# The first feed-forward layer of the last block as a 2x2 block product of seven multiplications, in the fused sliding-window attention and squared-ReLU kernel

## The chip, the cores and the metric

The kernel runs on one core of one Trainium2 chip. The metric is device time in microseconds (us) of one execution. The time before is 298.63 us, the median of 3 runs (298.5 to 298.88). The profile is of one more execution, which took 298.21 us; its span on the core's engines is 296.2 us, and the 2.0 us around the span are start and end of the program.

## The reference

`reference()` computes causal attention in a window of 64 positions, per head, then a feed-forward layer with a squared ReLU:

```python
scores = scale * np.matmul(q, k.transpose(0, 1, 3, 2))       # q, k, v: 8 batches, 8 heads, 576 positions, 64
scores = np.where((rel >= 0) & (rel < 64), scores, -1e9)     # rel = query position - key position
attn = softmax(scores); x = (attn @ v)                       # to 4608 tokens x 512
h = np.maximum(x @ w_in, 0.0)                                # w_in: 512 x 2048
out = (h * h) @ w_out                                        # w_out: 2048 x 512
```

Inputs and output are fp32; the kernel computes in fp16 with fp32 sums.

## The kernel before

The 4608 tokens are nine blocks of 512: block g takes positions 0 to 511 of batch g, and block 8 takes the last 64 positions of all eight batches. A block goes through three stages: attention in four units of two heads, which leaves its 512x512 input transposed in `xT[g]`; layer 1 (`F1`), which leaves the squared ReLU, features by tokens, in `h2[g]` (16 slices of 128 features); and layer 2, which writes the output. The stages of three blocks run beside each other: step n of the loop at L709 does layer 2 of block n, layer 1 of block n+1 and attention of block n+2. The order of every engine's queue is written out by hand: the body runs under `tc.manual_schedule()`, so each engine gets its instructions in program order, and it takes them one after the other.

**Layer 1** of a block is 16 calls of `F1` (L351). Each has four matmuls of 128x512 into one bank (L358, depth 512 in four chunks of 128), a maximum with zero on VectorE from the bank to an fp32 tile `hr` (L361), and a square on ScalarE into `h2` (L362). The banks are the two of the pool `ps_f1`, in turn.

**Layer 2** of blocks 2 to 8 is a 2x2 block product by seven multiplications already (`L2S`, L453), once for each half s of the tokens. A product p of 1 to 7 is eight matmuls of 128x256 (`product`, L446). Four sums of blocks of `h2` are formed for it by `S_sum` (L434, on VectorE at L422, 128x1024 fp16 each). Products add up in two banks: `chain` takes 1, 6, 7 and 4, one after the other, and `side` holds 2 in its left and 5 and 3 in its right half. After 1, 6, 5 and 4 ScalarE copies a result to the output tile (`scaled`, L460); after 2, 7 and 3 VectorE adds one to it (`plus`, L463). A product that goes on in `chain`, or starts anew in it, so waits until the copy or the addition before it has read the bank. In the last step (block 8) s=0 has the two `ps_f1` banks (`more`), and s=1 has `chain` and `side`.

**The order around the change.** For steps 1 to 8 a string (`order`, L726 to L728) says how calls of layer 1 ("1") and layer 2 ("2") follow each other; the resulting list is `fill`, and a place in it is called a position below. `put(i, work)` sets other work ahead of position i: sums, attention units, and so on (L733 to L761). Step 6 (layer 2 of block 6, layer 1 of block 7, attention of block 8) and step 7 (layer 2 of block 7, layer 1 of block 8, no attention) have 30 positions each, mostly "1" and "2" in turn. Step 8, the last, has only the 14 products of layer 2 of block 8. Sums that a step's first products need are formed at the end of the step before: `S_sum` 3 (position 20), 1 and 2 (positions 28 and 29) for s=0.

[...]

Of the kernel before, what the change touches and what calls it, by code (L numbers as in the profile page):

```python
# [8 lines left out]
FP32 = mybir.dt.float32  # L9
FP16 = mybir.dt.float16  # L10
# [5 lines left out]
def kernel(  # L16
# [314 lines left out]
    def X(g, hp, engine=nc.scalar, pool=ps_tr, tag="tr", own=None):  # L331

        if g not in xT:
            xT[g] = xtpool.tile([P, DMC, 512], FP16, name="xT", tag="xT")
        if g == B:
            nc.sync.dma_start_transpose(out=xT[g][:, hp, :].rearrange("p (j t) -> p j t", j=4),
                                        in_=xs[g, hp][:].rearrange("p j h d -> p (j h d)"))
            return
        if own is not None:
            tr = at_ps[own][:, 0, :].bitcast(FP16).rearrange("p (a b) -> p a b", a=2)  # L340
        else:
            tr = pool.tile([P, 2, 512], FP16, name="xtr", tag=tag)
        for jp in range(4):
            nc.tensor.transpose(out=tr[:, 0, jp * P:(jp + 1) * P], in_=xs[g, hp][:, jp, :, :],  # L344
                                identity=ident[:])
        copy(engine, xT[g][:, hp, :], tr[:, 0, :])
# [4 lines left out]
    def F1(g, f, pool=ps_f1, tag="f1", into=None):  # L351
        if g not in h2:
            h2[g] = h2pool.tile([P, FFC, 512], FP16, name="h2", tag="h2")
        hps, done = open_f1.pop((g, f), (None, 0))
        if hps is None:
            hps = into if into is not None else pool.tile([P, 512], FP32, name="hps", tag=tag)
        for c in range(done, DMC):
            nc.tensor.matmul(hps[:], w_in_sb[:, c, f * P:(f + 1) * P], xT[g][:, c, :],  # L358
                             start=(c == 0), stop=(c == DMC - 1))
        hr = opool.tile([P, 512], FP32, name="hr", tag="hr")  # L360
        nc.vector.tensor_scalar(out=hr[:], in0=hps[:], scalar1=0.0, scalar2=None, op0=ALU.max)  # L361
        nc.scalar.activation(out=h2[g][:, f, :], in_=hr[:], func=AF.Square)  # L362
# [58 lines left out]
    def minus(out, a, b, op=ALU.subtract, engine=None):  # L421
        (engine or nc.vector).tensor_tensor(out=out, in0=a, in1=b, op=op)  # L422
# [11 lines left out]
    def S_sum(g, k, s):  # L434
        if k == 1:
            minus(s_of(1, s), a_of(g, 1, 0, s), a_of(g, 1, 1, s), ALU.add)
        elif k == 2:
            minus(s_of(2, s), s_of(1, s), a_of(g, 0, 0, s))
        elif k == 3:
            minus(s_of(3, s), a_of(g, 0, 0, s), a_of(g, 1, 0, s))  # L440
        else:
            minus(s_of(4, s), a_of(g, 0, 1, s), s_of(2, s))

    def product(to, a, b, start):
        for f in range(HF):
            nc.tensor.matmul(to, a[:, f, :], b[:, f, :], start=start and f == 0, stop=f == HF - 1,  # L446
                             skip_group_check=True)

    def flush():
        while to_store:  # L450
            to_store.pop(0)()
# [65 lines left out]
    with tc.manual_schedule():  # L517
# [191 lines left out]
        for n in range(1, NBLK):  # L709
            g = seq[n]  # L710
            last = n == NBLK - 1
            one = None if last else seq[n + 1]
            if n == 1:
                second = [lambda ts=ts, i=i: F2(g, ts, i, None, None, into=(chain, side)[ts % 2])
                          for ts in range(4) for i in range(4)]
            elif last:
                more = [ps_f1.tile([P, 512], FP32, name="more", tag="f1") for _ in range(2)]
                banks = [(more[0][:, 0:HC], more[1]), (chain[:, 0:HC], side)]
                second = [lambda p=p, s=s: L2S(g, p, s, banks[s])
                          for p, s in ((1, 0), (2, 0), (1, 1), (6, 0), (2, 1), (5, 0), (7, 0),  # L720
                                       (6, 1), (3, 0), (4, 0), (5, 1), (7, 1), (3, 1), (4, 1))]
            else:
                second = [lambda p=p, s=s: L2S(g, p, s, (chain[:, 0:HC], side))
                          for s in range(2) for p in ORDER]
            first = [] if last else [lambda f=f: F1(one, f) for f in range(FFC)]
            order = ("22222222" + 8 * "112" if n == 1 else  # L726
                     "2" * 14 if last else
                     ("2112121212121211" if n == 2 else "1212121212121211") + "21212121121122")  # L728
            a, b = iter(first), iter(second)
            fill = [next(a if c == "1" else b) for c in order]  # L730
            at = {}

            def put(i, *work):  # L733
                at.setdefault(i, []).extend(work)

            if n == 1:
                put(0, lambda: Sc(g2, 3), lambda: A(g2, 2))
                put(2, lambda: M(g2, 3))
                put(3, lambda: X(g2, 2, own=1))
                put(5, lambda: A(g2, 3))  # L740
                put(7, lambda: X(g2, 3, own=1))
                for i, k in ((1, 1), (3, 2), (6, 3), (8, 4)):
                    put(i, lambda k=k: T_sum(k))
            else:
                for i, k, s in (((0, 1, 1), (0, 2, 1), (2, 4, 0), (3, 3, 1), (4, 4, 1)) if last else
                                ((2, 4, 0), (4, 1, 1), (6, 2, 1), (9, 3, 1), (18, 4, 1))):
                    put(i, lambda k=k, s=s: S_sum(g, k, s))
            if not last:
                end = len(fill) - 1
                put(24 if n == 1 else 20, lambda: S_sum(one, 3, 0))  # L750
                put(end if n == 1 else end - 1, lambda: S_sum(one, 1, 0))
                put(end, lambda: S_sum(one, 2, 0))
            base = 4 * (n + 2)
            for i, two in zip((11, 22) if n == 1 else (9, 20) if n == 2 else (9, 17) if n == 6 else (8, 19),
                              (units[base:base + 2], units[base + 2:base + 4])):
                for t, u in enumerate(two):
                    if u is not None:
                        put(i, lambda u=u, t=t: Sc(*u, i=t))
                        put(i + 3 + t, lambda u=u: M(*u))
                        put(i + 6, lambda u=u, t=t: A(*u, i=t))  # L760
                        put(i + (7 if u[0] == B else 8 + t), lambda u=u, t=t: X(*u, own=t))  # L761
            for i, group in enumerate(fill):
                for work in at.pop(i, []):
                    work()
                total = 12 + (30 * (n - 1) + i + 1) * (len(load_list) - 12) // 140
                while done < total and (parts_left or pending):
                    next_part()
                    done += 1
                group()
            assert not at, at.keys()  # L770
# [30 lines left out]
```

## Time and profile before

| what | value |
|---|---|
| profiled execution | 298.21 us, span 296.2 us |
| median of 3 runs | 298.63 us (298.5 to 298.88) |
| granted TensorE clock | 1.00 in every stage |
| step 7, 253.63 to 279.67 us | 26.04 us: TensorE busy 26.04, VectorE 18.05, ScalarE 12.37, GpSimd 0.00 |
| step 8, 279.67 to 292.06 us | 12.39 us: TensorE busy 12.39, VectorE 7.00, ScalarE 3.08, GpSimd 1.38 |
| tail, 292.06 to 296.2 us | 4.14 us: ScalarE 0.39, GpSimd 0.40, DMA |

The times of day in the text ("at 253.63") count from the start of the span. Steps are found in the trace by the matmuls: step 7 begins with the four matmuls into `hps` that follow product 4 of block 6, and step 8 with the first product into `more`. The profile's engines are PE (matmuls), PEld (loading of weights, beside PE), DVE (VectorE), ACT (ScalarE), POOL (GpSimd) and SP (the DMA queue). A line of a list of groups gives the line of the code, engine, operation, output and inputs with shapes and count, then total busy time and mean nanoseconds of one, then the idle time of the engine before them and who ended it. A line of a timeline gives start, length, engine, line and operation.

### The profile page before, as it was taken

To read this page: it belongs to the slowest core of one execution; us is meant where nothing else is said; L and a number is where in the kernel's file an instruction comes from. 1 tells how busy PE (TensorE), PEld (TensorE's weight loads), DVE (VectorE), ACT (ScalarE), POOL (GpSimd) and SP (SyncE) were. 2 spreads that over 40 slices of the span, in tenths; PEclk is the share of its full clock that TensorE was granted. 3 is DMA by queue.
4 is the path that set the end of the run, shared out by engine and by line. 5 is a ranking of instruction groups with operands and counts; after the bars stand their busy time and mean duration, and the time that the engine had idled before them with its cause. 6 is when DMAs were issued, how large, how long until landed. Compare 5 with 4: busy or idle time off the path is not lost.

```text
span 296.2 us, 7372 instructions
## 1 busy us (share of the span) xinstructions
PE 287.7 (97%) x2905; PEld 180.3 (61%) x2905; DVE 216.3 (73%) x379; ACT 170.3 (57%) x292; POOL 125.8 (42%) x215
## 2 busy tenths in 40 slices
PE   7899999999999999999999999999999999999994
PEld 5543545555445466667666766676667666766783
DVE  4677539588867787878778877987788679866651
ACT  3666757688366656565665566556655654444521
POOL 4668848984383267229425633913232000000002
PEclk9999999999999999999999999999999999999999
DMA  6999999999999995999999999799997023100015
GB/s 209 259 323 392 407 326 237 321 247 196 177 254 185 190 216 106 209 181 234 181 207 226 200 180 226 157 198 200 196 221 202 2 38 107 73 37 35 2 71 142
DMA packets 143650, 56.05 MB, mean 189 GB/s; under 512 B 127712, under 2 KB 136160, under 8 KB 143616
## 3 DMA queue, kind: packets, MB, share of 16 engines
q1 hardware_dynamic: 143232, 55.00, 85.2%
q0 software_dynamic: 144, 0.39, 0.6%
q8 instruction: 22, 0.36, 0.5%
q10 hardware_dynamic: 240, 0.20, 0.3%
q14 instruction: 12, 0.10, 0.1%
HBM read 38.80 MB, written 9.44 MB: 163 GB/s over the span
## 4 chain that ended last, share of the span: by engine, by line
PE 88%; SPq 5%; DMA 4%; POOL 1%; ACT 0%; issue 0%; DVE 0%
PE hps L358 39%; PE chain L446 16%; PE side L446 12%; PE ops L394 5%; DMA wsum<-in_moe_w_in_dram 4%; PE at L318 4%; PE at L288 3%; PE side L394 2%; PE chain L394 2%; SPq L180 2%; PE more L446 2%; PE at L344 2%; SPq L173 2%; PE tr L257 1%; SPq L132 1%; SPq L139 1%
## 5 line engine op out<-in xcount | busy, mean ns | idle before, releaser
L362 ACT ACTIVATE h<-hr 128x512 f16<-128x512 f32 x144 | 90.2, 630 | 92.5 <-DVE hr L361 92.1
L358 PE MATMUL hps<-xT,w_in_sb 128*128 128x512 f16 x560 | 138.6, 379 | 0.5 <-POOL w_in_sb L120 0.4
L361 DVE TENSOR_SCALAR hr<-hps 128x512 f32<-128x512 f32 x143 | 97.2, 687 | 42.6 <-PE hps L358 39.4
L358 PEld LDWEIGHTS <-w_in_sb 128*128 128x128 f16 x564 | 52.8, 98 | 48.1 <-POOL w_in_sb L120 1.9
L446 PEld LDWEIGHTS <-hsum 128*128 128x128 f16 x448 | 43.2, 98 | 13.2
L120 POOL CAST v_ev<-st_v 128x512 f16<-128x512 f32 x31 | 21.6, 696 | 45.3 <-DMA st_v<-in_v_dram 45.3
L446 PEld LDWEIGHTS <-h 128*128 128x128 f16 x336 | 32.7, 98 | 9.3
L120 POOL CAST k<-st_k 128x512 f16<-128x512 f32 x33 | 21.4, 651 | 38.2 <-DMA st_k<-in_k_dram 30.4
L295 ACT ACTIVATE pm<-at 128x1024 f16<-128x1024 f32 x35 | 34.1, 1014 | 2.1 <-PE at L288 2.1
L387 POOL DMA_DIRECT2D out_dram<-osb x3 | 1.8, 595 | 63.6 <-ACT osb L460 62.2
L446 PE MATMUL chain<-wsum,hsum 128*128 128x256 f16 x208 | 27.0, 273 | 0.0
L328 DVE TENSOR_TENSOR xs<-at,rden 128x512 f16<-128x512 f32 x36 | 24.9, 692 | 1.2
L302 DVE TENSOR_TENSOR pm<-pm,mask 128x1024 f16<-128x1024 f16 x32 | 23.7, 754 | 1.9 <-ACT pm L295 1.9
L422 DVE TENSOR_TENSOR hsum<-h 128x1024 f16<-128x1024 f16 x28 | 20.4, 728 | 5.4 <-ACT h L362 5.4
L233 POOL CAST v_od<-st_v 64x512 f16<-64x512 f32 x30 | 22.4, 748 | 1.6
L120 POOL CAST q<-st_q 128x512 f16<-128x512 f32 x28 | 19.2, 711 | 4.7 <-DMA qT<-q 2.1
L394 PEld LDWEIGHTS <-h 128*128 128x128 f16 x128 | 11.6, 98 | 12.2
L460 ACT ACTIVATE osb<-chain 128x256 f32<-128x256 f32 x39 | 14.5, 373 | 5.6 <-PE chain L446 5.6
L318 PEld LDWEIGHTS <-pm 128*64 128x64 f16 x576 | 11.2, 110 | 6.9 <-DVE pm L302 3.2
L118 ACT ACTIVATE xT<-at 128x512 f16<-128x512 f16 x22 | 12.8, 587 | 4.0 <-PE at L344 4.0
L394 PE MATMUL ops<-w_out_sb,h 128*128 128x512 f16 x64 | 14.8, 380 | 0.0
L318 PE MATMUL at<-v_ev,pm 128*64 128x65 f16 x384 | 13.8, 197 | 0.2 <-ACT v_ev L118 0.2
(91 smaller groups left out, 317.2 us busy)
## 6 DMA issues: line engine op xcount, KB each, us to landing
st_k<-in_k_dram SPq DMA_DIRECT2D x37, 256.0 KB, 3.7
out_dram<-osb SPq DMA_DIRECT2D x32, 256.0 KB, 2.8
st_q<-in_q_dram SPq DMA_DIRECT2D x29, 256.0 KB, 4.9
st_v<-in_v_dram SPq DMA_DIRECT2D x28, 256.0 KB, 4.1
w_st<-in_moe_w_in_dram SPq DMA_DIRECT2D x4, 512.0 KB, 5.9
wsum<-in_moe_w_in_dram SPq DMA_DIRECT2D x4, 512.0 KB, 9.8
hsum<-in_moe_w_out_dram SPq DMA_DIRECT2D x4, 512.0 KB, 7.9
wsum<-in_moe_w_out_dram SPq DMA_DIRECT2D x4, 512.0 KB, 9.2
```

Of the source, the lines that this page charges most:

```text
L120: engine.tensor_copy(out=out, in_=in_)
L233: nc.gpsimd.tensor_copy(out=od[g][to:to + 64, m, :, 0:D], in_=st["v", g, c][of:of + 64, :].rearrange("p (h d) -> p h d", h=H))
L295: nc.scalar.activation(out=p[:, hh, :] if apart else p[:], in_=sc[hh] if apart else both[:], func=AF.Exp, scale=1.0 / float(D) ** 0.5)
L302: nc.vector.tensor_tensor(out=p[:], in0=p[:], in1=m.unsqueeze(1).broadcast_to([P, 2, 512]), op=ALU.min)
L318: nc.tensor.matmul(a[jj * 64:(jj + 1) * 64, hh, jp * VW:jp * VW + D + 1], pm[g, hp][:, hh, j * 64:(j + 1) * 64], vsel, start=True, stop=True)
L328: nc.vector.tensor_tensor(out=x[:].rearrange("p j h d -> p h j d"), in0=a[:, :, :, 0:D], in1=rden[:].unsqueeze(3).broadcast_to([P, 2, 4, D ...
L358: nc.tensor.matmul(hps[:], w_in_sb[:, c, f * P:(f + 1) * P], xT[g][:, c, :], start=(c == 0), stop=(c == DMC - 1))
L361: nc.vector.tensor_scalar(out=hr[:], in0=hps[:], scalar1=0.0, scalar2=None, op0=ALU.max)
L362: nc.scalar.activation(out=h2[g][:, f, :], in_=hr[:], func=AF.Square)
L394: nc.tensor.matmul(f2[g, ts][:], h2[g][:, f, ts * P:(ts + 1) * P], w_out_sb[:, f, :], start=(f == 0), stop=(f == FFC - 1))
L422: (engine or nc.vector).tensor_tensor(out=out, in0=a, in1=b, op=op)
L446: nc.tensor.matmul(to, a[:, f, :], b[:, f, :], start=start and f == 0, stop=f == HF - 1, skip_group_check=True)
```

## The change

Layer 1 of block 8, in step 7, becomes a 2x2 block product: features in two halves i, depth (the 512 inputs) in two halves k, tokens in two halves j of 256. It needs four sums of blocks of `w_in` (`W_sum`, each two operations of 128x1024 fp16) and four of blocks of `xT` (`X_sum`, 128x512 fp16). W sums 1 and 2 are formed on GpSimd and sum 3 on VectorE, in step 6; X sum 1 in step 6, the others and W sum 4 in step 7, on VectorE.

A product p is made for one m of 0 to 3 at a time, which stands for two of the eight slices of 128 features of each half: four matmuls of 128x256 into one bank (`product1`). So there are 28 calls of `L1S`, in step 7's string "112" fourteen times, 42 positions: position 3k and 3k+1 hold product number k for two m side by side, and position 3k+2 a product of layer 2. Positions 0 to 20 are m of 0 and 1, positions 21 to 41 are m of 2 and 3, with products in the order 5, 1, 2, 6, 7, 3, 4.

Each m has three banks, a and b in its `at_ps` tile and c from `ps_f1`; even and odd m have different ones. Partial sums go from bank to bank by copies on ScalarE: product 5 in b is copied to SBUF (`kept5`), product 1 in a is copied to b, a takes product 2 on top and is finished (VectorE maximum, ScalarE square, `done`), b takes 6 and is copied to c, c takes 7, is copied to a, and is finished with `kept5` added; b takes 3 and is finished with `kept5` added; a takes 4 and is finished. To finish with `kept5` (`done5`) is an addition on VectorE, a maximum on GpSimd, and a square on GpSimd, or on ScalarE for the block (0, 1) of m 2 and 3.

In step 8 the second and third products change places ((1, 1) stands ahead of (2, 0), as p and s), and the sums of `h2` are formed in another order; sum 3 for s=0 of block 8 is formed in step 8, no more in step 7.

```diff
@@ -445,6 +445,93 @@
         for f in range(HF):
             nc.tensor.matmul(to, a[:, f, :], b[:, f, :], start=start and f == 0, stop=f == HF - 1,
                              skip_group_check=True)
+
+    wsums, xsums = {}, {}
+    HX = 256
+
+    def w_of(i, k):
+        return w_in_sb[:, 2 * k:2 * k + 2, i * HF * P:(i + 1) * HF * P]
+
+    def x_of(g, k, j):
+        return xT[g][:, 2 * k:2 * k + 2, j * HX:(j + 1) * HX]
+
+    def W_sum(k, engine, cc):
+        if k not in wsums:
+            t = tpool.tile([P, HP, 512], FP16, name="wS", tag="T")
+            wsums[k] = t[:].rearrange("p a b -> p (a b)").rearrange("p (c f) -> p c f", c=2)
+        a, b, op = {1: (w_of(1, 0), w_of(1, 1), ALU.add), 2: (wsums.get(1), w_of(0, 0), ALU.subtract),
+                    3: (w_of(0, 0), w_of(1, 0), ALU.subtract), 4: (w_of(0, 1), wsums.get(2), ALU.subtract)}[k]
+        minus(wsums[k][:, cc, :], a[:, cc, :], b[:, cc, :], op, engine)
+
+    def X_sum(g, k):
+        if k not in xsums:
+            t = apool.tile([P, 2, 512], FP16, name="xS", tag="pm", bufs=4)
+            xsums[k] = t[:, 0, :].rearrange("p (c t) -> p c t", c=2)
+        a, b = {1: (x_of(g, 0, 1), x_of(g, 0, 0)), 2: (x_of(g, 1, 1), xsums.get(1)),
+                3: (x_of(g, 1, 1), x_of(g, 0, 1)), 4: (x_of(g, 1, 0), xsums.get(2))}[k]
+        minus(xsums[k], a, b)
+
+    def product1(to, m, a, b, start):
+
+        for u in range(2):
+            f = (2 * m + u) * P
+            for cc in range(2):
+                nc.tensor.matmul(to[:, u * HX:(u + 1) * HX], a[:, cc, f:f + P], b[:, cc, :],
+                                 start=start and u == 0 and cc == 0, stop=cc == 1, skip_group_check=True)
+
+    kept5 = {}
+
+    def L1S(g, p, m, banks):
+
+        if g not in h2:
+            h2[g] = h2pool.tile([P, FFC, 512], FP16, name="h2", tag="h2")
+        a, b, c = banks
+
+        def h_of(i, j):
+            return h2[g][:, i * HF + 2 * m:i * HF + 2 * m + 2, j * HX:(j + 1) * HX]
+
+        def piece32(name):
+            return stp.tile([P, 512], FP32, name=name, tag="st")
+
+        def done(i, j, bank):
+            hr = piece32("ls")
+            nc.vector.tensor_scalar(out=hr[:], in0=bank, scalar1=0.0, scalar2=None, op0=ALU.max)
+            nc.scalar.activation(out=h_of(i, j), in_=hr[:].rearrange("p (u t) -> p u t", u=2), func=AF.Square)
+
+        def done5(i, j, bank):
+            y = piece32("ls")
+            nc.vector.scalar_tensor_tensor(out=y[:], in0=bank, scalar=1.0, in1=kept5[m][:],
+                                           op0=ALU.mult, op1=ALU.add)
+            nc.gpsimd.tensor_scalar(out=y[:], in0=y[:], scalar1=0.0, scalar2=None, op0=ALU.max)
+            y = y[:].rearrange("p (u t) -> p u t", u=2)
+            if m < 2 or j == i:
+                nc.gpsimd.tensor_tensor(out=h_of(i, j), in0=y, in1=y, op=ALU.mult)
+            else:
+                nc.scalar.activation(out=h_of(i, j), in_=y, func=AF.Square)
+
+        if p == 5:
+            product1(b, m, wsums[1], xsums[1], True)
+            kept5[m] = piece32("p5")
+            copy(nc.scalar, kept5[m][:], b)
+        elif p == 1:
+            product1(a, m, w_of(0, 0), x_of(g, 0, 0), True)
+            copy(nc.scalar, b, a)
+        elif p == 2:
+            product1(a, m, w_of(0, 1), x_of(g, 1, 0), False)
+            done(0, 0, a)
+        elif p == 6:
+            product1(b, m, wsums[2], xsums[2], False)
+            copy(nc.scalar, c, b)
+        elif p == 7:
+            product1(c, m, wsums[3], xsums[3], False)
+            copy(nc.scalar, a, c)
+            done5(1, 1, c)
+        elif p == 3:
+            product1(b, m, wsums[4], x_of(g, 1, 1), False)
+            done5(0, 1, b)
+        else:
+            product1(a, m, w_of(1, 1), xsums[4], False)
+            done(1, 0, a)
 
     def flush():
         while to_store:
@@ -717,14 +804,22 @@
                 more = [ps_f1.tile([P, 512], FP32, name="more", tag="f1") for _ in range(2)]
                 banks = [(more[0][:, 0:HC], more[1]), (chain[:, 0:HC], side)]
                 second = [lambda p=p, s=s: L2S(g, p, s, banks[s])
-                          for p, s in ((1, 0), (2, 0), (1, 1), (6, 0), (2, 1), (5, 0), (7, 0),
+                          for p, s in ((1, 0), (1, 1), (2, 0), (6, 0), (2, 1), (5, 0), (7, 0),
                                        (6, 1), (3, 0), (4, 0), (5, 1), (7, 1), (3, 1), (4, 1))]
             else:
                 second = [lambda p=p, s=s: L2S(g, p, s, (chain[:, 0:HC], side))
                           for s in range(2) for p in ORDER]
-            first = [] if last else [lambda f=f: F1(one, f) for f in range(FFC)]
+            apart = n == NBLK - 2
+            if apart:
+                cs = [ps_f1.tile([P, 512], FP32, name="c", tag="f1") for _ in range(2)]
+                three = [(at_ps[i][:, 0, :], at_ps[i][:, 1, :], cs[i][:]) for i in range(2)]
+                first = [lambda p=p, m=m: L1S(one, p, m, three[m % 2])
+                         for two in ((0, 1), (2, 3)) for p in (5, 1, 2, 6, 7, 3, 4) for m in two]
+            else:
+                first = [] if last else [lambda f=f: F1(one, f) for f in range(FFC)]
             order = ("22222222" + 8 * "112" if n == 1 else
                      "2" * 14 if last else
+                     "112" * 14 if apart else
                      ("2112121212121211" if n == 2 else "1212121212121211") + "21212121121122")
             a, b = iter(first), iter(second)
             fill = [next(a if c == "1" else b) for c in order]
@@ -742,13 +837,15 @@
                 for i, k in ((1, 1), (3, 2), (6, 3), (8, 4)):
                     put(i, lambda k=k: T_sum(k))
             else:
-                for i, k, s in (((0, 1, 1), (0, 2, 1), (2, 4, 0), (3, 3, 1), (4, 4, 1)) if last else
+                for i, k, s in (((1, 3, 0), (2, 1, 1), (3, 2, 1), (4, 4, 0), (6, 3, 1), (8, 4, 1)) if last else
+                                ((4, 4, 0), (8, 1, 1), (12, 2, 1), (17, 3, 1), (30, 4, 1)) if apart else
                                 ((2, 4, 0), (4, 1, 1), (6, 2, 1), (9, 3, 1), (18, 4, 1))):
                     put(i, lambda k=k, s=s: S_sum(g, k, s))
             if not last:
                 end = len(fill) - 1
-                put(24 if n == 1 else 20, lambda: S_sum(one, 3, 0))
-                put(end if n == 1 else end - 1, lambda: S_sum(one, 1, 0))
+                if not apart:
+                    put(24 if n == 1 else 20, lambda: S_sum(one, 3, 0))
+                put(end if n == 1 or apart else end - 1, lambda: S_sum(one, 1, 0))
                 put(end, lambda: S_sum(one, 2, 0))
             base = 4 * (n + 2)
             for i, two in zip((11, 22) if n == 1 else (9, 20) if n == 2 else (9, 17) if n == 6 else (8, 19),
@@ -759,6 +856,16 @@
                         put(i + 3 + t, lambda u=u: M(*u))
                         put(i + 6, lambda u=u, t=t: A(*u, i=t))
                         put(i + (7 if u[0] == B else 8 + t), lambda u=u, t=t: X(*u, own=t))
+            if n == NBLK - 3:
+                for i, k, engine in ((18, 1, pool), (18, 2, pool), (27, 3, dve)):
+                    for cc in range(2):
+                        put(i + (cc if engine is dve else 0), lambda k=k, e=engine, cc=cc: W_sum(k, e, cc))
+                put(25, lambda: X_sum(seq[-1], 1))
+            if apart:
+                for i, k in ((0, 2), (2, 3), (4, 4)):
+                    put(i, lambda k=k: X_sum(one, k))
+                for cc in range(2):
+                    put(5 + cc, lambda cc=cc: W_sum(4, dve, cc))
             for i, group in enumerate(fill):
                 for work in at.pop(i, []):
                     work()
```

## The prediction

> **What bounds the kernel now.** I read the busy times of the page first, then the chain that ended last, then the timeline of TensorE around the change, and last the groups of the other engines by shape.
>
> ```profile
> PE 287.7 (97%) x2905; PEld 180.3 (61%) x2905; DVE 216.3 (73%) x379; ACT 170.3 (57%) x292; POOL 125.8 (42%) x215
> ...
> PE 88%; SPq 5%; DMA 4%; POOL 1%; ACT 0%; issue 0%; DVE 0%
> ```
>
> TensorE (PE) is busy for 97% of the span and is 88% of the chain, so a matmul less is time less, and a wait of PE is time more. In steps 7 and 8 no PE instruction waits: what follows is judged only by the matmul time removed and the waits that PE gets.
>
> ```profile
> 276.20 1.89 PE L358 MATMUL hps<-xT,w_in_sb 128*128 128x512 f16 x8
> 277.92 1.04 PE L446 MATMUL side<-w_out_sb,hsum 128*128 128x256 f16 x8
> 278.80 1.04 PE L446 MATMUL chain<-wsum,h 128*128 128x256 f16 x8
> 279.67 1.91 PE L446 MATMUL more<-w_out_sb,h 128*128 128x256 f16 x16
> 281.42 1.04 PE L446 MATMUL chain<-w_out_sb,h 128*128 128x256 f16 x8
> ```
>
> Read the starts, not the lengths: a group's length holds about 0.17 us of drain beside the next group. Eight 512-wide matmuls take 277.92 - 276.20 = 1.72 us; sixteen 256-wide take 281.42 - 279.67 = 1.75, so 0.109 each. Step 7 takes 26.04 us (253.63 to 279.67), of which layer 2's 112 matmuls are 112 x 0.109 = 12.2; layer 1's 64 are the other 13.8 (0.216 each).
>
> **What the change saves.** Seven products of four m of four 256-wide matmuls are 112 x 0.109 = 12.2 us in place of 13.8: **1.6 us less**. Loading weights takes 98 ns in its rows, under 109, and stays covered. PE's work in step 8 is as long as before.
>
> **What it adds on the other engines.**
>
> ```profile
> L362 ACT ACTIVATE h<-hr 128x512 f16<-128x512 f32 x144 | 90.2, 630 | 92.5 <-DVE hr L361 92.1
> L460 ACT ACTIVATE osb<-chain 128x256 f32<-128x256 f32 x39 | 14.5, 373 | 5.6 <-PE chain L446 5.6
> ...
> L398 ACT ACTIVATE osb<-ops 128x512 f32<-128x512 f32 x4 | 2.4, 597 | 4.0 <-PE ops L394 4.0
> ```
>
> ```profile
> L361 DVE TENSOR_SCALAR hr<-hps 128x512 f32<-128x512 f32 x143 | 97.2, 687 | 42.6 <-PE hps L358 39.4 <-ACT xT L118 1.3 <-ACT h L362 0.7
> ...
> L422 DVE TENSOR_TENSOR hsum<-h 128x1024 f16<-128x1024 f16 x28 | 20.4, 728 | 5.4 <-ACT h L362 5.4
> L463 DVE SCALAR_TENSOR_TENSOR osb<-side,osb 128x256 f32<-128x256 f32 x26 | 10.9, 419 | 2.0 <-PE side L446 1.6 <-DMA out_dram<-osb 0.2
> ```
>
> ```profile
> L120 POOL CAST v_ev<-st_v 128x512 f16<-128x512 f32 x31 | 21.6, 696 | 45.3 <-DMA st_v<-in_v_dram 45.3
> ...
> L120 POOL CAST w_in_sb<-wsum 128x512 f16<-128x512 f32 x8 | 4.7, 613 | 0.9 <-DMA wsum<-in_moe_w_in_dram 0.6
> ...
> L88 POOL TENSOR_SCALAR maskb<-mask 128x448 f16<-128x448 f32 x1 | 1.3, 1322 | 0.0
> ```
>
> Back to back, an instruction starts some 0.03 to 0.05 after the length of the one before has nearly run out (two L361 in 1.28), so I count in queues: a 512-wide maximum or addition on VectorE (DVE) 0.65, a 1024-wide sum 0.64 (0.68 alone in step 7), an X sum half as wide 0.36 (0.68, less 512 at the 0.52 ns per element between the 1024- and 2048-wide sums), `plus` 0.38, a square on ScalarE (ACT) 0.60, `scaled` 0.36. A copy from bank to bank has no row; the nearest is L398, bank to SBUF, 0.60, and I take 0.57; half of that and twice that are its ends.
>
> All this work fits: in step 7 ACT goes from 12.4 to about 8 x 0.36 + 16 x 0.57 + 10 x 0.6 = 18 us of 24.5, DVE from 18.0 to about 19, POOL from 0 to some 15. W sums 1 and 2 (four operations of POOL, in program order at step 6's position 18) can run early: POOL's last cast of the whole trace ends at 227.1, and step 7 begins at 253.6. They cost nothing unless they hold DVE up; bounds 0 and 0.5 us.
>
> What matters is therefore the **order** in each queue. A triple (two products of 0.436, one of layer 2 of 0.871) takes 1.742 us. A bank's result is there 0.61 after its product starts (0.436 and the drain), and the next product of the same m starts 1.742 after. So a copy has 1.1 us for waiting and running, and needs 0.57. Three places exceed this.
>
> *Position 12, the first product 7.* Its bank c is filled by ACT's copy after product 6. On ACT that copy stands behind the two squares of product 2 (positions 6, 7), and these wait for DVE's maxima, which stand behind DVE's new sums. DVE around the start of step 7 in the trace of before:
>
> ```profile
> 250.41 0.42 DVE L463 SCALAR_TENSOR_TENSOR osb<-chain,osb 128x256 f32<-128x256 f32 x1
> 251.22 0.69 DVE L361 TENSOR_SCALAR hr<-hps 128x512 f32<-128x512 f32 x1 [0.38 <-PE hps L358]
> 252.15 0.69 DVE L361 TENSOR_SCALAR hr<-hps 128x512 f32<-128x512 f32 x1 [0.24 <-PE hps L358]
> 253.54 0.69 DVE L422 TENSOR_TENSOR hsum<-h 128x1024 f16<-128x1024 f16 x1 [0.69 <-ACT h L362]
> ```
>
> Its gaps here are 0.2 to 0.7; X sum 1 takes the first. From 251.22 on the queue holds two maxima (1.30), W sum 3 (1.28), two S sums (1.28), a `plus` (0.38), X sums 2, 3, 4 (1.08), S sum 4 (0.64), W sum 4 (1.28) and a `plus` (0.38): 7.62, so it is through at 258.84. Product 2's first result is there at 253.63 + 2 x 1.742 + 0.61 = 257.72, so the maxima run 1.1 late, to 260.13; the second square ends at 260.75, `scaled` at 261.1, the copy at 261.7. Product 7 was due at 253.63 + 4 x 1.742 = 260.60: PE waits 1.1, and 0.1 more for its neighbour. **+1.2** (0 if DVE is free, 1.9 with whole lengths in place of spacings).
>
> *Position 23, product 1 of layer 2 for s=1.* It starts `chain` anew and waits for the `scaled` of position 20. Count from the start of product 3 (position 15): its additions on DVE end at 1.26 and 1.90, S sum 3 of position 17 at 2.55, `plus` at 2.93, product 4's maxima at 3.58 and 4.2, its second square on ACT at 4.85, and behind it `scaled` at 5.2. Position 23 is due at 2 x 1.742 + 0.872 = 4.36. **+0.85** (0.2 without the S sum, 1.5 if DVE is late).
>
> *Step 8's second product, (1, 1).* The same, with POOL in the path. (2, 0) stood here before; now (1, 1) starts `chain` only 0.871 after position 41 ended. Count from product 3 of m 2. POOL's queue has maximum and square for (1, 1) of m 2, the same for m 3, then the two maxima for (0, 1): four maxima and two squares from about -0.5, when DVE's first addition after product 7 is done. A maximum lies between a cast's 0.61 and the 1.48 that L88's row gives per element for 512; I take 0.70, the casts in company with DVE, since they have this shape. A square reads two inputs, which no POOL row does: between one cast, 0.61, and twice L88, 3.0; I take two casts, 1.3. So POOL ends at -0.5 + 2.8 + 2.6 = 4.9. ACT takes its instructions in order: the square of (0, 1) of m 3, the two squares of product 4, `scaled`: 3 x 0.6 + 0.37 = 2.2 later, 7.1. (1, 1) is due at 4.36. **+2.7** (1.0 with everything on POOL at 0.61; 9 with L88 and 3.0). The S sums of step 8 come out of the same queue by 6.6, before the product that needs them; the reordering costs nothing else.
>
> [...]
>
> **Sum**, against the profiled execution: 298.21 - 1.6 + 1.2 + 0.85 + 2.7 = 301.4. The runs' median is 0.4 above that execution, so I forecast **301.8**.
>
> **Rivals.**
>
> *The gain comes through*: 298.6 - 1.6 = **297.0**. The two sets of banks then hide every copy. It decides at one point: POOL must be through the maximum of m 3 no later than 2.1 after product 3's start, so that `scaled` is done by 4.36. For it speaks that every engine has free time on average; against it that six operations even at the fastest cast take 3.7 from -0.5 on.
>
> *Even*: DVE has no backlog, a copy is faster, POOL is as fast as a cast: -1.6 + 0 + 0.2 + 1.0, **298.2** (298 to 299.2).
>
> *Copy and addition on bank c in turn*: after product 7 ACT copies c while DVE reads it. If one waits for the other, DVE starts 0.57 later, and POOL with it: **302.4**. No row of before has two engines on one bank. [...]
>
> *POOL as slow as L88*: four at 1.48, two at 1.48 to 3.0, the last wait 6.2 to 9: **305.3 to 308**. That row has a broadcast input and half the casts' rate, which speaks against it.
>
> **How the numbers follow.** Forecast 0.47 (own range 299.3 to 304), in turn 0.14, POOL slow 0.08, even 0.14, gain through 0.17. The range must take in all but 2 in 10: it leaves out most of the gain and the worst POOL, 298.0 to 305.5. A measurement can tell about 0.2% (0.6 us) from no change. Faster: the gain and a little of even, 0.19; same 0.08; slower 0.73.
>
> **What would show it.** In the changed trace: PE's step 7 has 224 matmuls at 0.109 and gaps ahead of the first product 7 (into c), of position 23 and of (1, 1); the last of these the longest, with ACT's `scaled` as releaser, and ACT's square before it waiting for POOL. DVE is busy without a gap from 251 to 260. I am wrong if POOL's two-input square takes under 0.8, if ACT runs the squares of product 4 ahead of those that wait for POOL, or if PE has no wait over 0.3 in step 7.

## The result and the profile after

The changed kernel takes **309.12 us** (median of 6 runs, 306.68 to 312.41), against 298.6 before (6 runs): a ratio of 1.0327, with a 95% interval of 1.0278 to 1.0375. The ratio is taken without the longest run, which is 1.9% above the shortest. The forecast was 301.8, with a range of 298.0 to 305.5: the direction held, the size did not. The profiled execution took 309.99 us, with a span of 308.3.

The page of the changed kernel, busy times and the clock granted in 40 slices:

```profile
PE 290.2 (94%) x2953; PEld 185.8 (60%) x2953; DVE 225.3 (73%) x387; ACT 174.3 (57%) x302; POOL 154.8 (50%) x233
...
PEclk9999999999999999999999999999999999999689
```

TensorE (PE) falls from 97% to 94% busy, and near the end the clock is granted only in part (6 and 8 tenths in two slices), which it was not in the kernel before (1.00 over the whole span). Where the 12.1 us of span are, by the starts of the matmuls in the two traces (the last matmul itself is 0.27 us in both):

| part | before | changed | difference |
|---|---|---|---|
| start of the span to step 7 | 253.63 | 255.85 | +2.22 |
| step 7 | 26.04 | 27.66 | +1.62 |
| step 8, start of its first to start of its last matmul | 12.12 | 20.29 | +8.17 |
| after the end of the last matmul | 4.17 | 4.20 | +0.03 |

The chain of waits in order of time (start, length, what ran) shows step 8 directly:

```profile
279.33 0.70 DVE ls L503
280.04 0.08 issue
280.12 1.49 POOL ls L505
281.61 0.07 issue
281.68 1.04 POOL h L508
282.72 1.46 POOL ls L505
284.18 0.07 issue
284.26 1.04 POOL h L508
285.29 2.91 POOL ls L505 x2
288.23 0.03 ACT h L510
...
288.76 1.13 ACT h L499 x2
289.90 0.28 ACT osb L547
290.17 0.04 issue
290.21 1.86 PE chain L446 x8
292.08 3.26 PE more L446 x16
295.34 0.87 PE side L446 x8
```

From 280.12 to 288.2 the end hangs on GpSimd (POOL), which works with pauses under 0.1: two times maximum and square, then two maxima. Behind it come ScalarE's squares (L510, then L499 for product 4) and the copy out of `chain` (L547), and only then PE may start (1, 1). It was due at 284.38 and began at 290.21: a wait of 5.8 us. The next line is a second cost: eight matmuls take 1.86 us where they took 0.87, and sixteen 3.26 instead of 1.75, until at 295.34 a product is 0.87 again. These are lengths in the chain, in which each piece begins where the one before it ends. The stretches around it, by engine, show why (start:end, length, busy times, granted clock):

```profile
283.51:284.40 0.89, 0.89 (x10) 0.78 (x8) 0.17 (x1) 0.00 (x0) 0.81 (x2) 1.00 0.62 230
284.40:290.20 5.80, 0.15 (x2) 0.00 (x0) 1.28 (x2) 2.60 (x6) 3.79 (x3) 0.83 0.00 0
290.20:295.10 4.90, 4.88 (x24) 3.37 (x24) 2.53 (x6) 0.62 (x2) 0.00 (x0) 0.50 0.14 54
295.10:304.10 9.00, 8.98 (x82) 7.81 (x80) 3.73 (x8) 1.92 (x5) 1.45 (x3) 1.00 0.27 60
```

The column ahead of the last two is the clock: 1.00, then 0.83 on average while PE is idle, 0.50 for the three products that follow, and 1.00 again. Step 8's 8.17 us are 5.83 of waiting and 2.34 that the matmuls take longer at half clock.

Step 7 without waits would be 24.42, by the prediction's own count (224 matmuls at 0.109). It is 27.66. The gaps between starts of matmuls, beyond a matmul's own time, are 0.96 ahead of the first product 6 (position 9), 0.75 ahead of product 5 of m 2 (21), 0.50 at position 23, and 0.16 each at positions 10, 19, 22 and 40: 2.85 of the 3.24. The rest is gaps of 0.04 to 0.12 at five more positions. The first of them in the timeline, then VectorE's queue just ahead of it:

```profile
260.21 1.04 PE L446 MATMUL chain<-wsum,hsum 128*128 128x256 f16 x8
262.05 1.20 PE L479 MATMUL at<-xS,wS 128*128 128x256 f16 x8 [0.80 <-DVE ls L498]
263.08 1.04 PE L446 MATMUL side<-wsum,hsum 128*128 128x256 f16 x8
264.07 1.08 PE L479 MATMUL c<-xS,wS 128*128 128x256 f16 x8
```

```profile
260.72 0.68 DVE L422 TENSOR_TENSOR wS<-w_in_sb,wS 128x1024 f16<-128x1024 f16 x1
261.31 1.28 DVE L498 TENSOR_SCALAR ls<-at 128x512 f32<-128x512 f32 x2
```

PE was free for product 6 at 261.09, and waited for VectorE's (DVE) maxima of product 2 (L498), which stood behind W sum 4. Product 7, into c, then came almost at its time (264.07, where 263.95 was possible).

The 2.22 us ahead of step 7 are two things. About 0.86 arose in the first 8 us, where the second load of q landed at 7.44 in place of 6.57, though it was issued at the same time. This is chance: at 214 us, up to where the programs are the same, the twelve traces of the change and its variants lie between 0.97 ahead of the trace before and 0.89 behind it. The other 1.36 arose between 227 and 241; first the changed kernel, then two of VectorE's sums before:

```profile
227.65 4.66 POOL L422 TENSOR_TENSOR wS<-w_in_sb 128x1024 f16<-128x1024 f16 x2
227.73 2.59 DVE L422 TENSOR_TENSOR hsum<-h,hsum 128x1024 f16<-128x1024 f16 x1
...
232.26 5.10 POOL L422 TENSOR_TENSOR wS<-wS,w_in_sb 128x1024 f16<-128x1024 f16 x2
232.78 0.68 DVE L361 TENSOR_SCALAR hr<-hps 128x512 f32<-128x512 f32 x1
233.38 2.00 DVE L422 TENSOR_TENSOR hsum<-hsum,h 128x1024 f16<-128x1024 f16 x1
```

```profile
227.11 0.68 DVE L422 TENSOR_TENSOR hsum<-h,hsum 128x1024 f16<-128x1024 f16 x1
...
230.03 0.68 DVE L422 TENSOR_TENSOR hsum<-hsum,h 128x1024 f16<-128x1024 f16 x1
```

While GpSimd forms W sums 1 and 2, VectorE's own sums of two inputs take 2.59 and 2.00 us, where they took 0.68; a maximum that reads a bank (L361) between them keeps its 0.68.

### The profile page after: what moved, and what is told of

Same layout as the page of the kernel before. It is cut to its first block, busy times and chain, and to the rows that moved or that the text cites. A ratio compares the mean times of both kernels' runs of the same rounds, so it can differ in the third digit from the quotient of the medians.

```text
span 308.3 us, 7522 instructions
## 1 busy us (share of the span) xinstructions
PE 290.2 (94%) x2953; PEld 185.8 (60%) x2953; DVE 225.3 (73%) x387; ACT 174.3 (57%) x302; POOL 154.8 (50%) x233
## 5 line engine op out<-in xcount | busy, mean ns | idle before, releaser
L362 ACT ACTIVATE h<-hr 128x512 f16<-128x512 f32 x128 | 80.1, 630 | 80.7 <-DVE hr L361 80.5
L358 PE MATMUL hps<-xT,w_in_sb 128*128 128x512 f16 x496 | 122.6, 379 | 1.0 <-DVE hr L361 0.6
L361 DVE TENSOR_SCALAR hr<-hps 128x512 f32<-128x512 f32 x127 | 86.0, 686 | 32.6 <-PE hps L358 30.2
L358 PEld LDWEIGHTS <-w_in_sb 128*128 128x128 f16 x500 | 46.6, 98 | 44.1 <-issue 2.3
L120 POOL CAST v_ev<-st_v 128x512 f16<-128x512 f32 x31 | 23.3, 752 | 43.3 <-DMA st_v<-in_v_dram 43.3
L422 DVE TENSOR_TENSOR hsum<-h 128x1024 f16<-128x1024 f16 x28 | 23.5, 841 | 9.8 <-ACT h L510 5.2
L505 POOL TENSOR_SCALAR ls<-ls 128x512 f32<-128x512 f32 x8 | 12.3, 1540 | 32.0 <-DVE ls L503 32.0
L120 POOL CAST q<-st_q 128x512 f16<-128x512 f32 x28 | 18.3, 676 | 5.8 <-DMA qT<-q 3.0
L446 PE MATMUL chain<-w_out_sb,h 128*128 128x256 f16 x104 | 14.3, 283 | 6.0 <-ACT osb L547 6.0
L547 ACT ACTIVATE osb<-chain 128x256 f32<-128x256 f32 x39 | 14.5, 372 | 5.7 <-PE chain L446 5.3
L550 DVE SCALAR_TENSOR_TENSOR osb<-side,osb 128x256 f32<-128x256 f32 x26 | 10.9, 418 | 6.0 <-ACT at L118 3.9
```

What stands on the lines that cost most here:

```text
L120: engine.tensor_copy(out=out, in_=in_)
L505: nc.gpsimd.tensor_scalar(out=y[:], in0=y[:], scalar1=0.0, scalar2=None, op0=ALU.max)
```

## The experiments

The **queue theory** says that the times come from what stands ahead in the queues of GpSimd, VectorE and ScalarE, each taken in order. Its first rival, the **bank theory**, puts the long wait down to (1, 1) having been moved ahead of (2, 0) onto a bank just left. All ratios are to the kernel before, run on the same chip.

**e1: two maxima from GpSimd to VectorE.**

```diff
-            nc.gpsimd.tensor_scalar(out=y[:], in0=y[:], scalar1=0.0, scalar2=None, op0=ALU.max)
+            (nc.vector if m >= 2 and j != i else nc.gpsimd).tensor_scalar(
+                out=y[:], in0=y[:], scalar1=0.0, scalar2=None, op0=ALU.max)
```

> The maximum of the block (0, 1) of m 2 and 3 is taken by VectorE, no more by GpSimd. Queue theory: the 5.7 us that TensorE waits ahead of step 8's second product come from GpSimd's four maxima (1.48 each) and two squares (1.04 each), behind which ScalarE's squares and the copy out of chain stand. Two of the maxima are taken off that path, so the wait falls to about 1 to 1.5, the granted clock stays at 1.00, and the time falls by 6 to 8 us, to 301 to 303. Bank theory (the wait is there because (1, 1) was moved ahead of (2, 0) onto the bank that product 4 just left): the wait stays over 4, and the time over 305.

Measured: 302.62 us, ratio 1.0148 (1.0095 to 1.0200). The wait ahead of (1, 1) is 0.86, the half clock is gone from step 8, and step 8 takes 12.98 in place of 20.29. Step 7 grows by 0.46, since product 4 of m 3 now waits 0.63 for VectorE. So one small edit of the queues takes 6.85 us off the two steps; the bank theory would have left the wait.

**e2: the order of step 8's products undone.**

```diff
-  for p, s in ((1, 0), (1, 1), (2, 0), (6, 0), (2, 1), (5, 0), (7, 0),
+  for p, s in ((1, 0), (2, 0), (1, 1), (6, 0), (2, 1), (5, 0), (7, 0),
```

> Step 8's second and third products stand as in the kernel before, (2, 0) ahead of (1, 1); all else as changed. Queue theory: (2, 0) needs the last squares of product 4, which stand behind the same GpSimd queue, 0.3 to 0.5 us ahead of the copy out of chain; the wait moves to (2, 0) and stays at 5 to 5.7, the time between 306 and 310. Bank theory: the wait falls under 2 and the time to 301 to 303.

Measured: 308.27 us, ratio 1.0361 (1.0293 to 1.0429). The wait only changes its product and its releaser:

```profile
PE more L446 <- ACT h L499: 4.5, 1, 4.5
```

(2, 0) into `more` now waits 4.5 us for the squares of product 4, which stand behind GpSimd's work as the copy did; this is somewhat less than the expected 5 to 5.7. The bank theory falls.

**e3: the wait filled with matmuls.** Between (1, 0) and (1, 1) stand 24 more matmuls whose result nobody reads.

```diff
+                if last and i == 1:
+                    for _ in range(24):
+                        nc.tensor.matmul(at_ps[0][:, 0, :], ident[:], w_in_sb[:, 0, 0:512], start=True, stop=True)
```

> Between the first and the second product of step 8, 24 matmuls of 128x512 are added (5.2 us of TensorE) into a bank that nothing reads; the output is unchanged. If the half clock after the wait (290.2 to 295.4) comes from TensorE standing idle, the granted clock stays 1.00, the products of step 8 keep 0.109 per matmul, and the time falls by about 2.4 us, to 306 to 307, although TensorE has more to do. If the half clock has another cause (the new products, or power), it stays, and the time is 309 or more.

Measured: 306.62 us, ratio 1.0286 (1.0240 to 1.0331). The interval overlaps that of the changed kernel, so the trace decides: with more work on PE, step 8 takes 17.95 in place of 20.29, and (1, 1) still starts 5.83 us after (1, 0) has ended. The filled wait and what follows it:

```profile
282.15:288.30 6.15, 6.15 (x34) 3.13 (x32) 0.90 (x3) 2.06 (x4) 4.61 (x4) 1.00 0.09 34
288.30:300.10 11.80, 11.31 (x104) 10.06 (x103) 6.80 (x13) 3.09 (x9) 1.30 (x2) 1.00 0.25 65
```

The clock stays at 1.00, where the changed kernel had 0.83 in its 5.8 idle us and 0.50 in the 4.90 behind them. So the half clock came here from PE standing idle, not from the new products. What sets its length was not tested: by the traces' clock records it lasted 6.8 us in the changed kernel and 3.4 in e2, e4 and e10, whose waits are 4.0 to 5.8. Equal waits can cost differently: e4 waits 5.84 as the changed kernel waits 5.83, but loses 1.33 to the half clock and not 2.34. In e2 and e10 matmuls had run again for 0.7 and 0.8 us before the half clock began; why it still came is open. The granted clock of the changed kernel's runs, 0.993 and 0.994 in the two shortest and 0.989 in the other four, suggests that a part of their spread is this; it is not shown, since only one of them has a trace.

**e4: W sums 1 and 2 on VectorE.**

```diff
+            if n == NBLK - 4:
+                for i, cc in ((20, 0), (27, 1)):
+                    put(i, lambda cc=cc: W_sum(1, dve, cc))
             if n == NBLK - 3:
-                for i, k, engine in ((18, 1, pool), (18, 2, pool), (27, 3, dve)):
-                    for cc in range(2):
-                        put(i + (cc if engine is dve else 0), lambda k=k, e=engine, cc=cc: W_sum(k, e, cc))
+                for i, k, cc in ((8, 2, 0), (11, 2, 1), (27, 3, 0), (28, 3, 1)):
+                    put(i, lambda k=k, cc=cc: W_sum(k, dve, cc))
```

> W sums 1 and 2 are formed on VectorE (four operations of 128x1024, two in step 5, two in step 6), no more on GpSimd. Theory: GpSimd's four operations (2.33 and 2.57 us) hold up VectorE's own sums of two inputs (2.6 and 2.0 in place of 0.68 in the changed trace), and TensorE lost about 1.3 us by it between 227 and 240. VectorE's sums then all take 0.7 or less in steps 5 and 6, and the time falls by 1.0 to 1.5, less what 2.6 us more on VectorE cost (0 to 0.5): 307.5 to 308.5. Rival: the 1.3 us come from X sum 1, W sum 3 or the start of the program, and stay: 309 or more, since VectorE has more to do.

Measured: 308.11 us, ratio 1.0319 (1.0270 to 1.0368); beside the changed kernel's 309.12 that is as forecast, but within the spread of the runs. The trace is clearer. VectorE's sums between 215 us and the start of step 7, first in the changed kernel, then in e4:

```profile
L422 DVE TENSOR_TENSOR hsum<-h,hsum 128x1024 f16<-128x1024 f16 x2 | 3.3, 1635 | 0.0
L422 DVE TENSOR_TENSOR hsum<-hsum,h 128x1024 f16<-128x1024 f16 x2 | 2.8, 1382 | 0.0
```

```profile
L422 DVE TENSOR_TENSOR hsum<-h,hsum 128x1024 f16<-128x1024 f16 x2 | 1.4, 678 | 0.0
L422 DVE TENSOR_TENSOR hsum<-hsum,h 128x1024 f16<-128x1024 f16 x2 | 1.3, 674 | 0.0
```

From 1.64 and 1.38 us each to 0.68 and 0.67. What PE loses against the trace before, by the starts of the same matmuls from 214 to 242 us, agrees over all runs here: 0.65 to 1.46 us in the eight with W sums 1 and 2 on GpSimd (1.36 in the changed kernel), 0 to 0.2 in the four with them on VectorE (0.09 in e4). Why GpSimd's sums stretch VectorE's sum beside them to 2.59, and leave the maximum between at 0.68, was not tested.

**e5: VectorE's queue in step 7 reordered**, on top of e1.

```diff
-  ((4, 4, 0), (8, 1, 1), (12, 2, 1), (17, 3, 1), (30, 4, 1)) if apart else
+  ((11, 4, 0), (20, 1, 1), (22, 2, 1), (24, 3, 1), (30, 4, 1)) if apart else
...
-  for i, k in ((0, 2), (2, 3), (4, 4)):
+  for i, k in ((0, 2), (2, 3), (10, 4)):
...
-                    put(5 + cc, lambda cc=cc: W_sum(4, dve, cc))
+                    put(8 + cc, lambda cc=cc: W_sum(4, dve, cc))
```

> On top of e1, only the places of sums in VectorE's queue change in step 7: W sum 4 goes from positions 5 and 6 to 8 and 9, X sum 4 to 10, S sum 4 to 11, and S sums 1, 2 and 3 for s=1 to 20, 22 and 24. The maxima of product 2 then have only X sums 2 and 3 and one addition ahead of them, those of product 4 no sum. Queue theory: the waits ahead of the first product 6 (1.0) and of product 5 of m 2 (0.75) fall under 0.2, that of position 23 (0.5) shrinks with them, and the time falls by 1.5 to 2.3 against e1, to 300.3 to 301.1. Rival (the products wait for something in the banks, whatever VectorE's queue): the waits stay and the time stays at 302.6.

Measured: 299.72 us, ratio 1.0054 (1.0034 to 1.0074), 0.6 below the expected span of 300.3 to 301.1; the profiled run also began step 7 1.55 us sooner than that of e1, with the same program up to there. Step 7 goes from e1's 28.12 to 25.84, or 2.28 less; no wait for L498 is left, and 0.28 at position 23. What VectorE had ahead of the maxima was the cause of these waits. The 0.63 ahead of product 4 of m 3 and the 0.86 ahead of (1, 1) stay as in e1.

**e6: product 4 ahead of product 3 in layer 2 of block 7**, on top of e1.

```diff
-                          for s in range(2) for p in ORDER]
+                          for s in range(2) for p in ((1, 2, 6, 5, 7, 4, 3) if n == NBLK - 2 else ORDER)]
```

> On top of e1, layer 2 of block 7 makes product 4 ahead of product 3, so that chain is left a triple earlier at positions 17 and 38, and product 3 stands at 20 and 41. Queue theory: the wait of position 23 (0.5) and that of step 8's second product (0.9) vanish; that of the products 6 and 5 stays; the time falls by 1.0 to 1.5 against e1, to 301.1 to 301.6. If what is late is not the copy out of chain but the squares that the products read, the last wait only moves to (2, 0), and the time stays within 0.5 of e1.

Measured: 301.71 us, ratio 1.0111 (1.0083 to 1.0140), 0.9 less than e1. Less than expected: position 23 and (1, 1) no longer wait, and product 5 of m 2 waits 0.3 in place of 0.75, but product 4 of layer 2 now follows product 7 after one triple and waits 0.3 and 0.4 for VectorE's addition, and (6, 0) waits 0.6 for a sum.

**e7: all together**, with e4, e5, e6, and for m 2 and 3 the maxima on VectorE and ScalarE.

```diff
-            nc.gpsimd.tensor_scalar(out=y[:], in0=y[:], scalar1=0.0, scalar2=None, op0=ALU.max)
+            if m >= 2 and j != i:
+                nc.scalar.activation(out=y[:], in_=y[:], func=AF.Relu)
+            else:
+                (nc.vector if m >= 2 else nc.gpsimd).tensor_scalar(
+                    out=y[:], in0=y[:], scalar1=0.0, scalar2=None, op0=ALU.max)
```

> All together: W sums 1 and 2 on VectorE, VectorE's order of e5, product 4 ahead of 3, and for m 2 and 3 no maximum on GpSimd: that of (1, 1) on VectorE, that of (0, 1) on ScalarE ahead of its square. Queue theory: no wait of TensorE over 0.3 is left in steps 7 and 8, the 1.6 us of matmul time come through, and the time is 296.8 to 298.0 against 298.4 before. If two sets of banks cannot hide the copies, waits of 0.3 to 0.6 stay at every triple, and the time is over 299.

Measured: 298.53 us, ratio 0.9999 (0.9974 to 1.0025), between the two expectations. Step 8 is back at 12.12, but step 7 is 26.67: e6's new waits of 0.3 and 0.4 grew to 0.4 and 1.65; VectorE has more ahead of that addition.

```profile
PE chain L446 <- DVE osb L554: 1.7, 2, 1.5
```

**e8: the banks a of both m in one tile, the banks b in the other**, on top of e1. `at_ps[0]` and `at_ps[1]` are the two attention tiles, each of two banks.

```diff
-  three = [(at_ps[i][:, 0, :], at_ps[i][:, 1, :], cs[i][:]) for i in range(2)]
+  three = [(at_ps[0][:, i, :], at_ps[1][:, i, :], cs[i][:]) for i in range(2)]
```

> On top of e1, a of both m lies in one attention tile and b of both in the other, where each m had both of its banks in one tile; nothing else changes. If product 6 waits for the maximum of product 2 only because both banks are halves of one tile, its wait (1.0 ahead of the first, 0.2 ahead of the second) vanishes, and what VectorE is late then arrives through ScalarE's copy at position 12, as the prediction had it: 0.8 to 1.2 ahead of product 7, the time within 0.5 of e1. If product 6 needs that maximum for another reason, the wait stays at position 9.

Measured: 311.55 us, ratio 1.0425 (1.0389 to 1.0461). The expectation missed by 9 us. The wait of position 9 is gone, as it would be if the shared tile were its cause, but new ones come for the same reason: now the two m share tiles, and each product of the second m but product 7, which goes into c, waits for whatever reads the first one's bank, though the banks differ:

```profile
PE at L479 <- DVE ls L498: 4.8, 4, 1.3
PE at L479 <- DVE ls L503: 2.6, 2, 1.3
PE at L479 <- ACT c L118: 1.8, 2, 0.9
PE at L479 <- ACT p L118: 1.6, 2, 0.9
PE at L479 <- ACT at L118: 1.5, 2, 0.7
```

These are 12 waits at the pairs of products that use the two tiles. In them a write to one half of a tile is ordered behind the reads of the other half; in the change the same ties a and b of one m together.

**e9: e7 without e6, and another bank for step 8's half s=1.**

```diff
-                banks = [(more[0][:, 0:HC], more[1]), (chain[:, 0:HC], side)]
+                banks = [(more[0][:, 0:HC], more[1]), (at_ps[0][:, 0, 0:HC], side)]
```

> As e7, but layer 2 of block 7 keeps its order (product 3 ahead of 4), and in step 8 the half s=1 adds up in a bank of an attention tile that product 4 of m 2 has left, not in chain. In e7 product 4 waited 0.4 and 1.65 for VectorE's addition of product 7, which came a triple too soon. Queue theory: these two waits go, the second product of step 8 waits for nothing, position 23 keeps 0.3; of the 1.6 us of matmul time 1.2 come through: 296.8 to 297.4, a ratio of 0.995 to 0.998. If the gain of matmul time is not real, the ratio is 1.000 or more with no wait left in the trace.

Measured: 299.25 us, ratio 1.0022 (0.9999 to 1.0045). The waits of e7 are gone and step 8 is 12.12, but product 4 of m 2 (position 39) waits 1.4 for VectorE's addition on the other bank of its tile, so step 7 is 26.70. The expectation missed that wait.

**e10: ScalarE's squares of (0, 1) put behind those of product 4**, else the changed kernel.

```diff
-                nc.scalar.activation(out=h_of(i, j), in_=y, func=AF.Square)
+                late.append(lambda: nc.scalar.activation(out=h_of(i, j), in_=y, func=AF.Square))
...
+                if apart and i == 41:
+                    group()
+                    while late:
+                        late.pop(0)()
```

> The changed kernel, but ScalarE's two squares of block (0, 1) of m 2 and 3 come behind the squares of product 4 and the copy out of chain in its queue; GpSimd does what it did. If ScalarE's order alone makes step 8's second product wait, that wait falls from 5.7 to under 1 and none takes its place: 302 to 303. If what GpSimd makes is itself late, the wait moves to the fourth product, which needs the sum of the squares: GpSimd ends 8.1 after it starts, two squares and two sums later (2.6) the product can start, about 4 us after it is due: a wait of 3.5 to 4.5, 304 to 307.

Measured: 307.69 us, ratio 1.0342 (1.0294 to 1.0390). The time lies above the expected 304 to 307: by the trace 1.7 us of step 8 are half clock, which the expectation did not count. The wait moves to (6, 0), and its releaser is the sum that needs GpSimd's result:

```profile
PE more L446 <- DVE hsum L422: 3.8, 1, 3.8
```

So ScalarE's order only passed the delay on sooner. What GpSimd makes was late by itself.

**e11: ScalarE takes both maxima of m 2 and 3**, those of (1, 1) behind both copies of product 7; GpSimd squares (0, 1) of m 2 too; VectorE's addition of product 7 for s=1 comes behind those of product 3; else as e9.

```diff
+                if m < 2:
+                    nc.gpsimd.tensor_scalar(out=y[:], in0=y[:], scalar1=0.0, scalar2=None, op0=ALU.max)
+                else:
+                    nc.scalar.activation(out=y[:], in_=y[:], func=AF.Relu)
+                if m < 3 or j == i:
+                    nc.gpsimd.tensor_tensor(out=h_of(i, j), in0=v, in1=v, op=ALU.mult)
...
+            if g == seq[-2] and s == 1:
+                held.append(lambda: plus(dn[:, hi], c))
```

> As e9, but for m 2 and 3 both maxima are taken by ScalarE (for (1, 1) behind both copies of product 7), GpSimd squares three of the four blocks, and VectorE's addition of product 7 for s=1 comes behind those of product 3. In e9 the first product 4 of m 2 waited 1.4, because the other bank of its tile was still to be read by VectorE behind GpSimd's and its own maxima. Queue theory: that wait falls to 0.2 or less, some 0.5 of waits is left in steps 7 and 8, and 1.0 to 1.2 of the 1.6 us come through: ratio 0.996 to 0.997, 296.8 to 297.3. If the time stays at or above that of before with waits under 0.6 in the trace, something other than the waits takes the gain back.

Measured: 297.84 us, ratio 0.9989 (0.9969 to 1.0008). The trace has no wait over 0.3 in steps 7 and 8; step 7 takes 25.17 and step 8 12.12, together 0.87 less than before. The ratio's interval holds both this and no change: between runs of either kernel the times spread by over 2 us, more than there is to gain. So a version that beats the kernel before is likely by its trace, and not shown by its time.

## Why the prediction was wrong, point by point

**The saved matmul time: right.** The products run at 0.436, and in e11, with almost no waits, step 7 is 25.17 against 24.42 counted. 1.6 us was all there was to gain.

**Position 12, +1.2: right in cause and size, wrong in place.** VectorE's maxima were 1.36 late (261.31, with product 2 there at 259.95 by the prediction's 0.61), where 1.1 was counted. PE met this at position 9, where product 6 waits for the maximum itself (0.96 and 0.16), because a and b are halves of one tile (e8). The prediction let it go the long way, over ScalarE's copy. That way was as late: product 7 began 1.25 after its place in a step without waits (264.07 against 262.82), just behind that copy, which ended at 264.0. So the size is no luck; what the prediction lacked is the shorter way. The same tie put 0.75 and 0.16 ahead of the products 5 of m 2 and 3, which the prediction did not have.

**Position 23, +0.85: right in place**, and of the right kind: 0.50 there. With the 0.91 just ahead of it, in positions 21 and 22, it is 1.4.

**Step 8's second product, +2.7: the step that failed.** The mechanism is as forecast, link by link in the chain above; the size is not. GpSimd's maximum was taken at 0.70, from the casts "since they have this shape", and is 1.48; the square was taken at 1.3 and is 1.04. So 4 x 1.48 + 2 x 1.04 = 8.0 stood in place of 5.4. The row of the same operation, L88, had given 1.48 for 512 elements in the prediction (1.51 from its 1322 ns for 448), and was put aside for a row of another operation. The start adds 0.9: GpSimd began 0.37 after product 3 of m 2 and not 0.5 before it. One part of that is the rival "copy and addition on bank c in turn", which holds here: VectorE's first addition started at 279.33, when ScalarE's copy of the bank (278.65 to 279.23) was through, though the product had been there since 278.57. Against these 3.5 us, ScalarE needed 1.95 behind GpSimd in place of 2.2, and PE itself came 0.27 later. So the wait was 5.83 in place of 2.7.

**The half clock, 2.3 us: not in the prediction at all.** The price of a long wait was taken to be its length; at 4.0 us and more it had a second part here, and at up to 1.65 (e7) it had none. Where between these it begins was not measured.

**W sums 1 and 2 on GpSimd, "0 and 0.5 us": 1.36.** That they can run early was right, and did not help: they held up VectorE's own sums. The prediction had named this as the condition, and its sum then took it at nothing.

**A slip of the working.** An X sum, 0.68 less 512 elements at 0.52 ns, is 0.41 and not 0.36, and the trace has 0.42. It decides nothing.

**The sum.** -1.6 + 3.2 (gaps of step 7) + 5.8 + 2.3 + 1.4 (W sums) + 0.9 (chance, at the start) is 12.0 of the 12.1 us between the two spans. Of the rivals, "POOL as slow as L88" was nearest (305.3 to 308, given 0.08): it had the right maximum, a square that was too dear (1.48 and more), and no price for the clock and the W sums. What the prediction held against it, that L88 has a broadcast input, did not matter: the maximum without one is as slow.

**What stays open.** By its trace e11 gives back 0.87 of the 1.6. The other 0.73 are gaps ahead of matmuls: 0.16 and 0.28 at positions 19 and 23, and 0.05 to 0.11 each at positions 12, 13, 18 and 34. What makes the small ones was not tested.

## What to carry to other kernels

A product less on the bound engine is worth its matmul time only if no queue behind it grows: count, for each wait, all that stands ahead in every queue on the way, price each instruction by a row of the same operation on the same engine before one of the same shape, and check what else shares the tile. Here 1.6 us of matmul could be won, and a queue of six GpSimd instructions at the end of a step cost 8. A wait of the tensor engine as long as those of 4.0 to 5.8 us here should be priced with the half-clocked matmuls that followed them, 1.3 to 2.3 us more. And work on GpSimd that nobody waits for had a price too where VectorE formed sums of two SBUF tiles beside it, 1.36 us here.

## What the runs showed of the hardware that was not expected

GpSimd's maximum with a constant, 128x512 fp32 in place, takes 1.48 us (one of the eight 1.92), and its product of two tensors of that size, to fp16, 1.04: here the operation with one input is the dearer. The same maximum on VectorE takes 0.43 and 0.55 (e1). ScalarE's copy of 128x512 fp32 takes 0.55 to 0.59 from bank to bank, and 0.59 to SBUF. GpSimd's sums of 128x1024 fp16 take 2.1 to 2.6 each, and stretch a VectorE sum beside them from 0.68 to as much as 2.59. Waits of 5.8 (the changed kernel and e4), 4.6 (e2) and 4.0 us (e10) brought the half clock for 3.4 to 6.8 us; the 0.86 of e1 and the 1.65 of e7 did not.
